# Attention and a gated two-layer network in one kernel: where the weight pieces stand in ScalarE's queue, and two flips ahead of two scores

## The chip, the core and the metric

The kernel runs on one core of one Trainium2 chip. The metric is the device time of one execution in microseconds, lower is better. The engines are TensorE (PE, its weight loads PEld), VectorE (DVE), ScalarE (ACT), GpSimd (POOL) and the queue that issues most transfers (SP).

## The reference

```python
# q, k, v: (8, 8, 576, 64) f32; block = 64, causal by blocks
scores = scale * np.matmul(q, k.transpose(0, 1, 3, 2))
scores = np.where(block_i >= block_j, scores, -1e9)
attn = np.exp(scores - np.max(scores, axis=-1, keepdims=True))
attn = attn / (np.sum(attn, axis=-1, keepdims=True) + 1e-09)
x = np.matmul(attn, v)            # then (B, H, S, D) -> (4608, 512)
h = x @ w_in                      # (512, 2048)
g = h * (1.0 / (1.0 + np.exp(-1.702 * h)))
out = g @ w_out                   # (2048, 512), f32
```

The weights come in as 64-bit floats.

## The kernel before

**Attention.** The 64 (batch, head) pairs are taken two at a time, in 32 turns n = 0 to 31 (and a last one that only finishes). `HP` is 4, so turns 0 to 3 are the first batch and the fifth turn is n = 4. A turn cuts the 576 rows of queries into five chunks (0 of 64 rows, 1 to 4 of 128). `load` fetches q and k, `prep` transposes them on DVE (L297). `score` multiplies them on PE into PSUM banks, then for each chunk DVE adds the mask and takes the row maxima (`weigh`, L351), ACT takes the exponential and its row sums (L358), DVE turns the sums into factors (L368, L371) and POOL multiplies (L376). In the first eight turns the weights are transposed by `flip` on PE (L102) and copied back by ACT (L411, L424). `av` multiplies them with the values on PE; ACT copies the sums of values to `xr` (L451, L450).

**The list of a turn.** `ORDER`, `START` (for n = 4) and `HANDOVER` (n = 8) are lists of items: `1+0`, `2/3`, `4` are scores of those chunks of head pair n, `a` is the flip of chunks 0 and 1 of n, `B` the flip of chunks 2 and 3 of n - 1, `C` the flip of chunk 4 of n - 1, `V` is `av(n - 1)`, `L` is `prep(n + 1)`, and `-` is nothing. After each item `convert` and `advance` are called.

**The weights.** 32 pieces of 128 x 512 are made from 64-bit words to a high and a low part. `load_weights` fetches a piece, `begin` lets ACT write its low words, scaled, to the one PSUM bank of tag `w3` (L219), `merge` is three DVE instructions (L223, L229, L234), and `split_weights` is ACT's cast to the high part (L243) and POOL's subtraction for the low part (L82). `begin` of the next piece needs that bank back, so it waits for L234 of this one. `convert` is called with a target from `WEIGHTS_BY`, in half steps: an even one is `merge`, an odd one is `split_weights` of this piece, the load of another and `begin` of the next.

**The network.** `moe` takes 12 tiles of 384 rows of `xr`: `split` makes high and low parts (ACT L498, DVE L82), 16 column groups each multiply with `w_in`, pass the gate (ACT L562, DVE L563, ACT L571, POOL L82) and multiply with `w_out`. The first tile waits for the sums of the first four head pairs, which are complete after `V` of the fifth turn. `advance` hands out its PE work by the position of the turn.

**What orders the queues.** A scheduler in the framework places each engine's instructions when the program is built: the earliest in program order of those that it reckons ready. The chip then runs each engine's list in that order. `keep_in_program_order` puts an instruction behind the one that was traced just ahead of it on its engine; it doesn't hold back what comes later. All PE work is pinned so, and the first three loads of pieces. PSUM banks are handed out in rotation by `bank()`: seven before the network starts.

Of the kernel before, what the change touches and what calls it, by code (L numbers as in the profile page):

```python
# [13 lines left out]
AF = mybir.ActivationFunctionType  # L14
# [15 lines left out]
)  # L30

START = "1+0 - B 2/3 L C - V - 4 - a - - -"
HANDOVER = "B C - 3+0/2+1 - - V - - - 4 - - L - -"


WEIGHTS_BY = ((0, 0), (8, 13), (14.5, 32))
TILES_BY = ((8.4, 0), (17.7, 1), (33.7, 4), (65.7, -2))

# [2 lines left out]
def attention_moe_kernel(  # L41
# [9 lines left out]
    nc = tc.nc  # L51
    B, H, S, D = q.shape
# [11 lines left out]
    HP = H // 2  # L64
# [6 lines left out]
    def f(ap):  # L71
        return ap.bitcast(F32)
# [5 lines left out]
    def phase(n):  # L78
        return 0 if n < HP else 1 if n < 2 * HP else 2

    def subtract(eng, out, in0, in1):
        eng.tensor_tensor(out=out, in0=in0, in1=in1, op=ALU.subtract)  # L82
# [3 lines left out]
    turns = {"n": 0, "bank": 0, "experts": False}  # L86
# [37 lines left out]
    def weights(name, g):  # L124
        if (name, g) not in home:
            home[name, g] = room(f"{name}{g}", [P, 4, WC], F32R, name)
        return home[name, g]
# [33 lines left out]
    for i in range(NCH):  # L161
        w, o = BLK * (2 * i + 1), 2 * BLK * i * i
# [12 lines left out]
    pieces = []  # L175
# [11 lines left out]
    def load_weights(upto):  # L187
        while conv["loaded"] < min(upto, len(pieces)):
            j = conv["loaded"]
            if j < 2 * len(places):  # L190
                if j % 2 == 0:
                    pair_of[j // 2] = room(places[j // 2], [P, 2, 2 * WC], U32, "words")
                at = [pair_of[j // 2][:, j % 2]]
            else:
                at = [
                    room("e1", [P, WC], U32, "wst") if j % 2 and x
                    else d2.tile([P, WC], U32, tag="osb", name="wst", bufs=3)
                    for x in range(2)
                ]
            n = 2 * WC // len(at)  # L200
            for x, w in enumerate(at):
                d = nc.sync.dma_start(out=w, in_=pieces[j][0][:, x * n : (x + 1) * n])
                if j < 3:
                    tc.keep_in_program_order(d)
            parts[j] = [
                (w.rearrange("p (c t) -> p c t", t=2), slice(x * n // 2, (x + 1) * n // 2))
                for x, w in enumerate(at)
            ]
            conv["loaded"] += 1
# [3 lines left out]
    bits, whole = {}, {}  # L213

    def begin(j):

        bits[j] = ps.tile([P, 512], F32, tag="w3", name="wm")
        for w, c in parts[j]:
            nc.scalar.activation(out=bits[j][:, c], in_=f(w[..., 1]), func=AF.Copy, scale=2.0**-112)  # L219

    def merge(j):
        u = bits.pop(j).bitcast(U32)
        nc.vector.tensor_scalar(  # L223
            out=u, in0=u, scalar1=3, scalar2=None, op0=ALU.logical_shift_left
        )

        z = whole[j] = room("e1" if j % 2 and j < 2 * len(places) else "wm", [P, WC], U32, "wm")
        for w, c in parts[j]:
            nc.vector.scalar_tensor_tensor(  # L229
                out=u[:, c], in0=w[..., 1], scalar=0x80000000, in1=u[:, c],  # L230
                op0=ALU.bitwise_and, op1=ALU.bitwise_or,
            )
        for w, c in parts.pop(j):
            nc.vector.scalar_tensor_tensor(  # L234
                out=z[:, c], in0=w[..., 0], scalar=29, in1=u[:, c],
                op0=ALU.logical_shift_right, op1=ALU.bitwise_or,
            )

    def split_weights(j):
        _, name, g, x = pieces[j]  # L240
        z = whole.pop(j)
        hi, lo = (weights(name + p, g)[:, x] for p in "hl")
        nc.scalar.copy(out=hi, in_=f(z))  # L243
        subtract(nc.gpsimd, lo, f(z), f(hi))

    def convert(upto):

        while conv["step"] < int(2 * upto):
            j, odd = divmod(conv["step"], 2)
            if odd:  # L250
                split_weights(j)
                if j + 1 < len(pieces):
                    load_weights(j + 3)
                    begin(j + 1)
            else:
                if j == 0:
                    begin(0)
                merge(j)
            conv["step"] += 1
# [201 lines left out]
    def order(n):  # L461
        return {HP: START, 2 * HP: HANDOVER}.get(n, ORDER[phase(n)]).split()

    def step(n):

        turns["n"] = n
        now = n < NPAIR

        def item(x):
            if x == "V":  # L470
                return (lambda: av(n - 1)) if n else None
            if x == "L":
                return (lambda: prep(n + 1)) if n + 1 < NPAIR else None
            if x in ("a", "B", "C"):
                m, chunks = {"a": (n, [0, 1]), "B": (n - 1, [2, 3]), "C": (n - 1, [4])}[x]
                return (lambda: flip(m, chunks)) if m >= 0 else None
            return (lambda: score(n, [[int(z) for z in y.split("+")] for y in x.split("/")])) if now and x != "-" else None

        return [item(x) for x in order(n)]
# [29 lines left out]
    def moe():  # L509
# [24 lines left out]
        for t in range(NT):  # L534
# [6 lines left out]
            for fc in range(NFC):  # L541
                if t == 0:
                    convert(fc // FG * GROUP + NDC + fc % FG + 1)
# [38 lines left out]
    def quota(pos):  # L582
        xs, ys = zip(*TILES_BY)
        return -1.0 if pos < xs[0] else np.interp(pos, xs, [ends[y if y >= 0 else y - 1] for y in ys])
# [7 lines left out]
    def advance(heads_done, until):  # L592

        while not state["done"] and not (until() and (state["gate"] or turns["n"] <= 2 * HP)):
            if state["wait"] is not None:
                if heads_for(state["wait"]) > heads_done:
                    return
                state["wait"] = None
            got = next(mo, None)
            if got is None:  # L600
                state["done"] = True
            elif isinstance(got, tuple):
                if got[0] == "tile":
                    state["wait"] = got[1]
                else:
                    state["gate"] = True
            else:
                state["gate"] = False
                state["t"] += got
# [14 lines left out]
    for n in range(NPAIR + 1):  # L624
        items = step(n)
        for sl, fn in enumerate(items):
            if fn is not None:
                fn()
            if order(n)[sl] == "V":
                heads_done = 2 * n  # L630
            pos = 2 * (n + (sl + 1) / len(items))
            convert(min(len(pieces), np.interp(pos - 0.5, *zip(*WEIGHTS_BY))))
            lim = quota(pos)
            advance(heads_done, lambda: state["t"] >= lim)
    advance(2 * NPAIR, lambda: False)
# [29 lines left out]
```

## Time and profile before

| what | value |
|---|---|
| runs | 1115.9, 1118.8 and 1119.08 us, median 1118.8 |
| span of the profiled execution | 1116.9 us |
| PE busy | 1082.2 us, 97% |
| PEld, DVE, ACT, POOL busy | 82%, 52%, 45%, 36% |
| mean granted TensorE clock | 0.988 |

The profile gives the span from the first to the last instruction of one execution. What lay around it in that execution isn't listed; the span is within the spread of the runs, 1.9 us under their median. A matmul's end is modelled, so PE's busy time is an upper bound. The granted clock is a share of 2.4 GHz, and 0.50 is 1.2 GHz.

### The profile page before, as it was taken

Reading aid. Unit: us, or ns where it says so; the run is one execution under the profiler, and the core shown is the slowest. Engines: PE = TensorE matmul, PEld = TensorE weight load, DVE = VectorE, ACT = ScalarE, POOL = GpSimd, SP = SyncE. Lnnn points to the kernel's source line nnn. Section 1 sums busy time; section 2 is a strip of 40 time slices with the busy share of each in tenths; the row PEclk is TensorE's granted clock in tenths of the full one; section 3 lists DMA queues with packets and bytes.
Section 4 is the critical chain, followed back from the end, with each engine's and each line's share of the span. In section 5 each row is a group of like instructions: output and inputs, shape, how many; then the busy total and the mean of one; then the engine's idle time right before and its main releaser. Section 6 shows DMA issues by size and latency. Waiting matters only on the chain. (4 is left out here: it accounts for less than half of the span.)

```text
span 1116.9 us, 19972 instructions
## 1 busy us (share of the span) xinstructions
PE 1082.2 (97%) x6960; PEld 912.9 (82%) x6960; DVE 584.2 (52%) x1856; ACT 498.9 (45%) x1321; POOL 406.4 (36%) x509
## 2 busy tenths in 40 slices
PE   6979999999999999999999999999999999999998
PEld 4757777788888888888888888888888888899997
DVE  6786786655645645655555555645645654211210
ACT  5865775443533534534443443443444434322322
POOL 4665565332333333333333332333333333122222
PEclk8979999999999999999999999999999999999999
DMA  8634523342434433243443333344442332200000
GB/s 183 193 89 153 146 61 80 72 103 59 96 81 86 109 80 70 58 99 71 113 86 75 80 92 68 63 108 86 86 103 66 71 84 54 54 30 1 29 1 29
DMA packets 219365, 91.25 MB, mean 82 GB/s; under 512 B 197760, under 2 KB 197760, under 8 KB 219264
## 3 DMA queue, kind: packets, MB, share of 16 engines
q1 hardware_dynamic: 214528, 89.38, 34.1%
q8 instruction: 55, 0.90, 0.3%
q10 hardware_dynamic: 4736, 0.59, 0.3%
q14 instruction: 46, 0.38, 0.1%
HBM read 45.09 MB, written 9.44 MB: 49 GB/s over the span
## 5 line engine op out<-in xcount | busy, mean ns | idle before, releaser
L82 POOL TENSOR_TENSOR gl<-g,gh 128x384 fp32r<-128x384 f32 x192 | 194.5, 1013 | 555.1 <-ACT gh L571 450.4
L563 DVE SCALAR_TENSOR_TENSOR g<-g,hp 128x384 f32<-128x384 f32 x192 | 106.0, 552 | 318.6 <-ACT g L562 317.2
L99 PE MATMUL hp<-xh,wih 128*128 128x384 f32 x768 | 265.8, 346 | 2.8 <-DVE g L563 1.8
L562 ACT ACTIVATE g<-hp 128x384 f32<-128x384 f32 x192 | 94.2, 491 | 368.5 <-PE hp L99 361.0
L99 PE MATMUL hp<-xh,wil 128*128 128x384 f32 x768 | 258.7, 337 | 0.0
L99 PE MATMUL hp<-xl,wih 128*128 128x384 f32 x768 | 254.4, 338 | 0.2
L99 PE MATMUL acc<-woh,gh 128*128 128x512 f32 x576 | 233.9, 406 | 0.0
L99 PE MATMUL acc<-wol,gh 128*128 128x512 f32 x576 | 227.0, 394 | 0.0
L99 PEld LDWEIGHTS hp<-xh,wih 128*128 128x128 f32 x768 | 144.4, 188 | 30.9 <-DVE g L563 20.3
L99 PE MATMUL acc<-woh,gl 128*128 128x512 f32 x576 | 168.2, 393 | 0.3 <-POOL gl L82 0.3
L571 ACT CAST gh<-g 128x384 fp32r<-128x384 f32 x192 | 98.4, 513 | 156.8 <-DVE g L563 156.5
L99 PEld LDWEIGHTS hp<-xh,wil 128*128 128x128 f32 x768 | 144.6, 188 | 5.6
L358 ACT ACTIVATE e<-e,mx 64x64 f32<-64x64 f32 (+4 forms) x240 | 132.2, 552 | 32.2 <-DVE mx L351 32.2
L376 POOL TENSOR_TENSOR e<-e,sm 64x64 f32<-64x64 f32 (+1 forms) x192 | 113.6, 612 | 86.3 <-DVE sm L371 42.5
L99 PEld LDWEIGHTS hp<-xl,wih 128*128 128x128 f32 x768 | 144.0, 188 | 1.0 <-DVE xl L82 1.0
L99 PE MATMUL bank<-qk 64*128 64x320 f32 (+4 forms) x768 | 124.3, 432 | 16.2 <-DVE qk L297 10.4
L99 PEld LDWEIGHTS acc<-woh,gh 128*128 128x128 f32 x576 | 108.2, 188 | 34.2 <-issue 10.8
L99 PEld LDWEIGHTS acc<-woh,gl 128*128 128x128 f32 x576 | 107.6, 188 | 25.4 <-POOL gl L82 1.2
L351 DVE CUSTOM_DVE_ANT_0 e<-bank,mask 64x64 f32<-64x64 f32 (+4 forms) x240 | 89.7, 417 | 70.1 <-PE bank L99 67.0
L99 PEld LDWEIGHTS acc<-wol,gh 128*128 128x128 f32 x576 | 108.4, 188 | 16.8 <-issue 0.4
L385 DVE STREAM_TRANSPOSE turned<-e 128x384 f32<-128x384 f32 (+1 forms) x192 | 92.5, 500 | 49.5 <-POOL e L376 48.9
L99 PEld LDWEIGHTS bank<-qk 64*128 64x128 f32 x768 | 71.4, 196 | 56.4 <-issue 25.4
(50 smaller groups left out, 960.6 us busy)
## 6 DMA issues: line engine op xcount, KB each, us to landing
turned<-turned SPq DMA_DIRECT2D x192, 80.0 KB, 2.1
turned<-turned SPq DMA_DIRECT2D x96, 112.0 KB, 2.2
raw<-in_q_dram SPq DMA_DIRECT2D x128, 72.0 KB, 2.3
out_dram<-osb SPq DMA_DIRECT2D x36, 256.0 KB, 2.4
raw<-in_k_dram SPq DMA_DIRECT2D x120, 72.0 KB, 2.4
turned<-turned SPq DMA_DIRECT2D x96, 88.0 KB, 2.1
words<-in_moe_w_in_dram SPq DMA_DIRECT2D x16, 512.0 KB, 5.6
vp<-in_v_dram SPq DMA_DIRECT2D x60, 128.0 KB, 2.4
```

The source lines that it names most:

```text
L82: eng.tensor_tensor(out=out, in0=in0, in1=in1, op=ALU.subtract)
L99: return tc.keep_in_program_order(nc.tensor.matmul(**kw))
L351: nc.vector.tensor_tensor_reduce(out=e[0:m, hd, lo:hi], in0=s, in1=mk, op0=ALU.add, op1=ALU.min, scale=-0.125, scalar=3e38 if lo == 0 else ...
L358: nc.scalar.activation(out=e[0:m, hd], in_=e[0:m, hd], func=AF.Exp, scale=-1.0, bias=mx[0:m, i, hd : hd + 1], accum_out=sm[0:m, i, hd : hd ...
L376: nc.gpsimd.tensor_tensor(out=x, in0=x, in1=sc.to_broadcast([m, width(i)]), op=ALU.mult)
L385: nc.vector.transpose(out=tw[:, :, SLOT[i] : SLOT[i] + i, hd].rearrange("p b j c -> p j b c"), in_=e[:, hd, 0 : i * P],)
L562: nc.scalar.activation(out=g, in_=hp[:, 0:tt], func=AF.Tanh, scale=1.702)
L563: nc.vector.scalar_tensor_tensor(out=g, in0=g, scalar=1.0, in1=hp[:, 0:tt], op0=ALU.add, op1=ALU.mult)
L571: nc.scalar.copy(out=gh, in_=g)
```

## The change

- `begin`'s ACT instructions are pinned behind what was traced ahead of them on ACT, in the turns n = 0 to 4.
- In an odd half step, the load and `begin` of the next piece are traced ahead of this piece's cast and subtraction.
- In turns 0 to 3 `convert` isn't called after the items 5 to 9 of the list (`L C - 4 -`), so what it would have done there comes after `V`.
- In the fifth turn `B` comes ahead of `1+0`, and the list has 16 items in place of 15.

```diff
-START = "1+0 - B 2/3 L C - V - 4 - a - - -"
+START = "B 1+0 - - 2/3 L C - V - 4 - a - - -"
+HELD = (5, 10)
@@ def begin(j):
         for w, c in parts[j]:
-            nc.scalar.activation(out=bits[j][:, c], in_=f(w[..., 1]), func=AF.Copy, scale=2.0**-112)
+            b = nc.scalar.activation(out=bits[j][:, c], in_=f(w[..., 1]), func=AF.Copy, scale=2.0**-112)
+            if turns["n"] <= HP:
+                tc.keep_in_program_order(b)
@@ def convert(upto):
             if odd:
-                split_weights(j)
                 if j + 1 < len(pieces):
                     load_weights(j + 3)
                     begin(j + 1)
+                split_weights(j)
@@ for n in range(NPAIR + 1):
             pos = 2 * (n + (sl + 1) / len(items))
-            convert(min(len(pieces), np.interp(pos - 0.5, *zip(*WEIGHTS_BY))))
+            if n >= HP or not HELD[0] <= sl < HELD[1]:
+                convert(min(len(pieces), np.interp(pos - 0.5, *zip(*WEIGHTS_BY))))
```

## Rows read from the trace of the kernel before

**Rows 1.** Windows: stretch and length, busy of PE, PEld, DVE, ACT, POOL, clock, DMA.

```profile
9.60:60.00 50.40, 42.50 (x362) 31.34 (x358) 40.23 (x151) 39.44 (x124) 30.68 (x44) 0.90 0.69 178
60.00:90.00 30.00, 23.69 (x138) 17.96 (x139) 22.08 (x51) 18.77 (x50) 17.52 (x19) 0.72 0.34 83
90.00:215.00 125.00, 116.48 (x805) 92.78 (x802) 90.95 (x265) 82.50 (x217) 69.49 (x77) 1.00 0.40 106
215.00:1116.90 901.90, 897.11 (x5650) 768.79 (x5648) 428.53 (x1381) 356.13 (x930) 286.14 (x359) 1.00 0.32 72
```

**Rows 2.** Waits of PE, 0 to 220: releaser, total us, times, longest.

```profile
PE bank L99 <- DVE qk L297: 10.4, 3, 7.1
...
PE bank L102 <- ACT xr L450: 2.1, 1, 2.1
```

**Rows 3.** Timeline of PE, 55 to 79: start, length, instruction, count, [idle before].

```profile
57.11 0.87 PE L102 MATMUL bank<-ident,turned 128*128 128x128 f32 x6
60.51 1.33 PE L99 MATMUL bank<-qk 64*128 64x192 f32 x8 [2.52 <-DVE qk L297]
...
64.98 2.37 PE L102 MATMUL bank<-ident,turned 128*128 128x128 f32 x10 [2.10 <-ACT xr L450]
68.16 3.87 PE L99 MATMUL bank<-qk 64*128 64x320 f32 x8 [0.82 <-ACT turned L424]
```

**Rows 4.** Timeline of ACT, 59 to 68.

```profile
59.73 0.62 ACT L243 CAST woh<-wm 128x512 fp32r<-128x512 f32 x1 [1.82 <-DVE wm L234]
60.26 0.63 ACT L219 ACTIVATE wm<-words 128x512 f32<-128x512 f32 x1
63.18 0.62 ACT L243 CAST woh<-wm 128x512 fp32r<-128x512 f32 x1 [2.29 <-DVE wm L234]
...
64.26 0.58 ACT L451 COPY xr<-bank 128x512 f32<-128x512 f32 x1
...
66.61 0.62 ACT L243 CAST woh<-wm 128x512 fp32r<-128x512 f32 x1 [0.98 <-DVE wm L234]
67.13 0.62 ACT L219 ACTIVATE wm<-words 128x512 f32<-128x512 f32 x1
67.69 0.42 ACT L424 COPY turned<-bank 64x128 f32<-64x128 f32 x2
```

**Rows 5.** Timeline of DVE, 59 to 65.

```profile
59.70 0.75 DVE L297 STREAM_TRANSPOSE qk<-raw 128x576 f32<-128x576 f32 x1
60.92 0.70 DVE L223 TENSOR_SCALAR wm<-wm 128x512 uint32<-128x512 uint32 x1 [0.47 <-ACT wm L219]
...
64.35 0.70 DVE L223 TENSOR_SCALAR wm<-wm 128x512 uint32<-128x512 uint32 x1 [1.21 <-ACT wm L219]
```

**Rows 6.** Timeline of SP, then of ACT: the third piece's load and first instruction.

```profile
22.68 0.97 SPq L202 DMA_DIRECT2D words<-in_moe_w_in_dram  x2
...
46.04 0.64 ACT L219 ACTIVATE wm<-words 128x512 f32<-128x512 f32 x1
```

**Rows 7.** DVE's idle before L223, whole run: releaser, us, times.

```profile
  ACT wm L219: 15.8, 18
```

**Rows 8.** Timeline of PE: the third turn's scores of chunks 2 and 3.

```profile
36.33 1.98 PE L99 MATMUL bank<-qk 64*128 64x320 f32 x8
```

**Rows 9.** Windows again: around the stretch at the lower clock.

```profile
57.00:60.30 3.30, 0.99 (x14) 0.65 (x8) 3.30 (x7) 1.48 (x6) 2.44 (x4) 1.00 0.00 0
60.40:73.90 13.50, 10.48 (x39) 7.32 (x40) 10.55 (x32) 10.23 (x32) 8.29 (x10) 0.50 0.75 183
74.00:80.00 6.00, 5.07 (x71) 4.34 (x69) 4.85 (x10) 4.03 (x10) 4.72 (x5) 1.00 0.01 3
200.00:206.00 6.00, 3.40 (x15) 1.87 (x14) 4.83 (x15) 1.58 (x5) 2.06 (x3) 1.00 0.11 25
```

**Rows 10.** Timeline of DVE: the subtractions of the first and the second tile.

```profile
77.66 3.50 DVE L82 TENSOR_TENSOR xl<-xr,xh 128x384 fp32r<-128x384 f32 x4
...
202.29 1.96 DVE L82 TENSOR_TENSOR xl<-xr,xh 128x384 fp32r<-128x384 f32 x4
```

## The prediction, made before the changed kernel was run

> **What bounds the kernel now.** I cut the span into stretches first [rows 1]. From 215 us on PE is busy 897.11 of 901.90 us: the change has nothing to win there, and as PE's work is the same before and after, a late start is carried through to the end one for one. So the change is worth what it does to PE's idle time ahead of 215 us, and to the stretches in which its clock is low. Between 9.6 and 60 us PE is idle for 7.90 us (50.40 - 42.50), between 60 and 90 for 6.31, between 90 and 215 for 8.52: 22.73 us in all, the most that any new order could return apart from the clock.
>
> Then the waits of PE say for whom [rows 2]: q and k transposed by DVE 10.4 us (7.1 of it the start of the kernel, which stays), and once 2.1 us the copy of sums of values on ACT. The timeline of PE places them [rows 3]. The flips of chunks 0 and 1 of the fourth turn begin at 57.11 and last 0.87. Then the fifth turn's first scores wait 2.52 us for DVE, `B`'s last ten transposes wait 2.10 us for L450, and the scores of chunks 2 and 3 wait 0.82 us for L424. This is the jam that the change is aimed at: 5.44 us of waits in 10 us.
>
> ACT's timeline shows why L450 was late [rows 4]. ACT stood at the cast of one piece until 59.73, at that of the next until 63.18 (2.29 us idle), and only at 64.26 came L451, the copy of sums that PE had finished before it began the flips at 57.11. L424 then waited behind another cast, which held ACT for 0.98 us. Each cast waits for DVE's L234, and DVE in turn waited 0.47 and 1.21 us for ACT's L219 [rows 5]. The two engines hand one piece back and forth, and the rest of their lists stands behind it.
>
> **The pins.** I work out which `begin` they bind. `WEIGHTS_BY` gives 13 pieces in 8 units of position, a turn is 2 units, so 6.5 half steps a turn: after the fourth turn the program has 24 half steps, 12 merges. The trace lags far behind. ACT's third L219 runs at 46.04, though its load went out at 22.68 [rows 6], and the one at 60.26 is the sixth [rows 4]. The program has the sixth `begin` in half step 10, late in the second turn (position 3.58); what it is pinned behind ran long ago. The L451 that was late belongs to the fourth turn. So as far as the lag stays, the pins and the held items leave the jam's order as it is, and I cost them at nothing. What hides them is the lag; if it goes (the first two pieces are moved behind the first turn's last scores, which may shift everything after), they would put the two casts and L219s behind L451. That is the first rival.
>
> **The next piece ahead of the cast.** When L234 ends, ACT now runs L219 first and the cast second. From the row, cast to L219 is 0.53 us (59.73 to 60.26) [rows 4]: L219 comes that much sooner, the cast 0.6 us later. It helps where DVE stands at L223 for ACT, which it does 18 times, 15.8 us in all [rows 7]. In the jam: the first such wait is 0.47 us, all of it saved, the second 1.21 us, of which 0.53 is saved [rows 5]. L451 comes 0.47 us sooner and L424, behind one more piece, 1.0 us sooner. The scores of chunks 2 and 3 wait for L424 last, so **1.0 us** on the path (bounds 0, if DVE fills the time with other work, and 2.1, if four pieces each pass on 0.53). The later waits of L223 lie where PE has the network's work; of these, some 14 waits at 0.53 us or 7.4 us of DVE time, I take **0.5 us**, since only the 8.52 us of idle after 90 us [rows 1] can return any of it; bounds 0 and 4. The later cast puts POOL's low parts off by 0.6 us; no wait of PE for them is among the rows, so nothing, with 0.6 as the other bound.
>
> **B ahead of 1+0.** Before, PE had nothing from 57.98 (57.11 + 0.87) to 60.51. `B` needs only the fourth turn's weights, so ten of its transposes can run in that hole, and the last four wait for L451, because the rotation of seven banks brings them to the bank of the sums (two for the sums, two for the flips, three for `B`, then again the first). The first scores come after them. They lose nothing that counts: they were computed by 61.84, but the next scores are released by L424 at 67.69 + 0.42 in any case [rows 3, 4]. So the 2.52 and 2.10 us aren't given back as such; they lie beside the wait for ACT. What is gained is that ACT can copy `B`'s flips, three banks that the scores of chunks 2 and 3 need next, ahead of the fifth turn's exponentials. At half clock eight such scores need some 3.96 us (twice the 1.98 of the third turn [rows 8]) against 3.87 seen, so hardly any of that time was a wait: I take **0.3 us**, bounds 0 and 0.82.
>
> **The clock.** Between 57.0 and 60.3 PE was busy for 0.99 of 3.30 us, and from 60.4 to 73.9 the granted clock was 0.50, with PE busy 10.48 us; then it is 1.00 again [rows 9]. With ten transposes in the hole, PE is busy more just ahead of the fall. But it then stands until L451, so the fall can come later and not be avoided. The eight scores at 68.16 took 3.87 us, the same in the third turn at full clock 1.98 [rows 3, 8]: 1.9 us for these alone. I take **1.5 us**, as the low stretch is likelier shortened than not; bounds 0 and 5.2 (half of 10.48).
>
> The Trainium skill, GPSIMD Engine Reference, "1. Specifications", says that GpSimd's SBUF interface is shared with VectorE, and that instructions with two SBUF inputs contend. The rows agree: four L82 subtractions on DVE took 3.50 us where POOL was busy 4.72 of 6 us, and 1.96 where it was busy 2.06 [rows 9, 10]. By it, a cast that comes later moves POOL's subtraction under other work of DVE, and the sum would be smaller by up to 1.5 us.
>
> **The sum.** 1.0 + 0.5 + 0.3 + 1.5 = 3.3 us less. The span is 1116.9; the sum gives 1113.6 for it. What lies around it isn't listed, so I take the sum from the median of the runs, 1.9 above the span: 1118.8 - 3.3 = **1115.5 us**.
>
> **Rivals.**
> - *The sums really go first.* If the moved first pieces end the lag, L451 follows PE at once. Then all of 5.44 us goes, and with it most of the low clock, 2.9 us if eight scores (1.9) and ten transposes (1.0, of 2.37) run at full clock: 8.3 us less, 1110.5. For it: ACT did stand 2.29 us at one cast [rows 4]. Against: the count of half steps above.
> - *Nothing that can be measured.* The 0.53 us per piece is eaten by the rest of DVE's list, which in 9.6 to 60 is busy 40.23 of 50.40 [rows 1], and the clock falls all the same: 1118.8, within 0.3%. (0.3%, 3.4 us, is about what a measurement of this kernel can tell from no change; the runs before lie 3.2 apart.)
> - *The quicker pieces take DVE from the attention.* Old pieces stand ahead of everything in the list. If one more is merged ahead of the fifth turn's q and k at 59.70 [rows 5], that costs three instructions of 0.70, 2.1 us, on the wait that was 2.52, and the first scores, which now come behind `B`, lose their slack. With subtractions that fall under POOL as in [rows 10], 1.5 us, it is 3.6 us: 1122.4. It decides once the scores of chunks 2 and 3 start later than 68.16. For it: DVE was busy 3.30 of 3.30 us ahead of them [rows 9]. Against: DVE then stood idle for 0.47 and 1.21 us in the jam [rows 5].
>
> The skill's rule on the shared interface belongs to the last of these; the trace so far shows it at the tiles' subtractions alone.
>
> **How the numbers follow.** My forecast has 0.42; its own range is 1112.5 to 1118, so half of it lies beyond 0.3% (0.22 faster, 0.20 same). The sums first: 0.20, faster. Nothing: 0.20, same. DVE taken: 0.18, slower. Faster 0.42, same 0.40, slower 0.18. The range goes from somewhat under the first rival's 1110.5, since the clock's bound is 5.2, to just short of the last rival's 1122.4: 1109 to 1122.
>
> **What would show it.** In the changed trace, each L219 ahead of its cast by some 0.6 us, and DVE's 15.8 us at L223 down by a third or more. In the jam: `B`'s first ten transposes ahead of 60.5, L451 at about 63.8 (at 58 by the first rival), L424 ahead of 67, scores of chunks 2 and 3 at about 67, and a low clock of less than 13.5 us. The first tile's first matmul comes some 2.8 us sooner. I am wrong if the scheduler, seeing pieces sooner, orders the third and fourth turns anew, so that PE's 7.90 us of idle ahead of 60 grow, or if the idle time after 90 us changes by more than what happens ahead of it.

## The result: 0.45% slower, and the profile after

Seven runs of the changed kernel have a median of 1122.45 us (1119.64 to 1126.71), seven of the kernel before 1118.8 (1115.9 to 1119.65): ratio 1.0045, interval 1.0031 to 1.0059. (The ratio is not that of the medians, which lie 3.65 us or 0.33% apart; it is the measure used throughout.) The forecast was 1115.5 us with a range of 1109 to 1122. The median is 3.65 us higher where a gain of 3.3 was forecast.

The profiled execution took 1122.59 us, with a span of 1120.8 (before 1116.9). In the changed kernel each line number is 1 to 3 higher: L82 is now L83, L219 is L220, L223 is L226, L234 is L237, L243 is L246, L376 is L379, L411 is L414, L424 is L427 and L451 is L454. The experiments shift them again by a few.

Windows of the changed kernel, columns as in [rows 1]:

```profile
9.60:60.00 50.40, 40.34 (x374) 30.37 (x371) 39.15 (x154) 40.67 (x128) 31.77 (x45) 0.93 0.68 179
60.00:90.00 30.00, 24.07 (x146) 18.66 (x145) 26.08 (x62) 19.54 (x52) 18.78 (x20) 0.77 0.32 83
90.00:215.00 125.00, 114.78 (x759) 90.98 (x758) 87.27 (x248) 78.07 (x208) 66.82 (x74) 0.95 0.39 102
215.00:1120.80 905.80, 900.82 (x5677) 771.79 (x5675) 429.60 (x1387) 357.83 (x933) 287.13 (x360) 1.00 0.32 72
```

Against [rows 1], the first two stretches have higher clocks (0.93 for 0.90, 0.77 for 0.72) and more instructions of PE done. The third has 759 matmuls in place of 805, 10.22 us of idle time in place of 8.52, and a clock of 0.95 where it was 1.00. So in these two profiles time is gained early and lost between 90 and 215 us.

**The jam is relieved.** Timeline of PE, the stretch of [rows 3]:

```profile
56.81 1.97 PE L103 MATMUL bank<-ident,turned 128*128 128x128 f32 x16
59.83 0.63 PE L103 MATMUL bank<-ident,turned 128*64 128x128 f32 x4 [1.06 <-ACT xr L454]
60.39 0.76 PE L100 MATMUL bank<-qk 64*128 64x192 f32 x8
63.19 3.40 PE L100 MATMUL bank<-qk 64*128 64x320 f32 x8 [2.03 <-ACT turned L427]
```

Timeline of ACT, the stretch of [rows 4]:

```profile
58.11 0.62 ACT L246 CAST woh<-wm 128x512 fp32r<-128x512 f32 x1 [0.93 <-DVE wm L237]
58.64 0.62 ACT L220 ACTIVATE wm<-words 128x512 f32<-128x512 f32 x1
59.20 0.58 ACT L454 COPY xr<-bank 128x512 f32<-128x512 f32 x1
61.65 0.63 ACT L220 ACTIVATE wm<-words 128x512 f32<-128x512 f32 x1 [1.08 <-DVE wm L237]
62.22 0.60 ACT L246 CAST woh<-wm 128x512 fp32r<-128x512 f32 x1
62.73 0.41 ACT L427 COPY turned<-bank 64x128 f32<-64x128 f32 x2
```

The flips of `a` and the first ten of `B` run in one row of 16 from 56.81. ACT takes up one cast and one L220 and then the sums, at 59.20; before, two such pairs stood ahead of L451 at 64.26. At 61.65 the new order shows: L220 0.57 us ahead of its cast (at 58.11 the scheduler still put a cast first). The waits of 2.52, 2.10 and 0.82 us are gone, one of 1.06 and one of 2.03 stand in their place. The scores of chunks 2 and 3 start at 63.19 (before 68.16), and the first matmul of the network at 74.66 (before 78.32). DVE's idle time ahead of L226, whole run, as in [rows 7]:

```profile
  ACT wm L220: 10.2, 13
```

It was 15.8 us in 18 times.

**The loss at the eighth turn's flips.** `B` and `C` flip the weights of the turn before, so the eighth turn's flips (head pair n = 7) stand at the head of the ninth turn's list. "Eighth" below means these flips. Timeline of PE of the changed kernel, from `B`'s ten to the scores that follow (the last nine belong to `C`):

```profile
178.14 1.25 PE L103 MATMUL bank<-ident,turned 128*128 128x128 f32 x10
181.39 0.63 PE L103 MATMUL bank<-ident,turned 128*64 128x128 f32 x4 [2.00 <-ACT turned L414]
184.33 2.18 PE L103 MATMUL bank<-ident,turned 128*128 128x128 f32 x9 [0.89 <-POOL turned L379]
189.29 1.78 PE L100 MATMUL bank<-qk 64*128 64x448 f32 x10
```

The same of the kernel before:

```profile
180.61 1.25 PE L102 MATMUL bank<-ident,turned 128*128 128x128 f32 x10
182.35 0.63 PE L102 MATMUL bank<-ident,turned 128*64 128x128 f32 x4 [0.49 <-ACT turned L411]
185.16 1.20 PE L102 MATMUL bank<-ident,turned 128*128 128x128 f32 x9 [0.78 <-POOL turned L376]
188.05 1.78 PE L99 MATMUL bank<-qk 64*128 64x448 f32 x10
```

From these flips to these scores it is 7.44 us before (188.05 - 180.61) and 11.15 after (189.29 - 178.14). The 2.47 us by which the flips start sooner than before become a lag of 1.24. The same nine flips take 1.20 us before and 2.18 after: the clock. Windows of the changed kernel, the two late stretches at the lower clock:

```profile
182.00:188.80 6.80, 5.92 (x21) 4.75 (x20) 1.19 (x4) 2.15 (x6) 3.56 (x4) 0.50 0.00 0
205.90:212.70 6.80, 6.43 (x17) 5.28 (x18) 4.83 (x15) 2.25 (x5) 0.99 (x1) 0.50 0.13 22
```

The granted clock is 0.50 (1.2 GHz) in both; in the trace of before it is 1.00 in both windows. What held the four flips at 181.39 up, ACT's timeline of the changed kernel shows:

```profile
179.18 0.38 ACT L220 ACTIVATE wm<-wst 128x256 f32<-128x256 f32 x1
179.50 0.61 ACT L246 CAST woh<-wm 128x512 fp32r<-128x512 f32 x1
180.01 0.51 ACT L574 CAST gh<-g 128x384 fp32r<-128x384 f32 x1
180.42 0.40 ACT L220 ACTIVATE wm<-wst 128x256 f32<-128x256 f32 x1
180.75 1.33 ACT L414 COPY turned<-bank 128x512 f32<-128x512 f32 x3
```

The same of the kernel before:

```profile
181.31 0.50 ACT L571 CAST gh<-g 128x384 fp32r<-128x384 f32 x1
181.71 1.07 ACT L411 COPY turned<-bank 128x512 f32<-128x512 f32 x2
182.67 0.64 ACT L243 CAST woh<-wm 128x512 fp32r<-128x512 f32 x1
```

Before, only the gate's cast stood ahead of the first copy of flips, which began 1.10 us after the flips (181.71 - 180.61). After, L220, the cast of the last piece but one, the gate's cast and another L220 do, and it begins 2.61 us after them.

But the wait that ends last is the one for POOL, ahead of the nine flips. They need two multiplications (L376, now L379). Timeline of POOL of the changed kernel:

```profile
179.83 1.15 POOL L379 TENSOR_TENSOR turned<-turned,sm 128x576 f32<-128x576 f32 x1 [3.88 <-DVE sm L374]
180.93 1.28 POOL L83 TENSOR_TENSOR wol<-wm,woh 128x512 fp32r<-128x512 f32 x1
182.16 1.01 POOL L83 TENSOR_TENSOR gl<-g,gh 128x384 fp32r<-128x384 f32 x1
183.12 1.15 POOL L379 TENSOR_TENSOR turned<-turned,sm 128x576 f32<-128x576 f32 x1
```

The same of the kernel before:

```profile
181.89 1.01 POOL L82 TENSOR_TENSOR gl<-g,gh 128x384 fp32r<-128x384 f32 x1 [2.66 <-ACT gh L571]
182.85 2.25 POOL L376 TENSOR_TENSOR turned<-turned,sm 128x576 f32<-128x576 f32 x2
```

After the change the piece's subtraction (its low part, 1.28 us) and the gate's stand between the two multiplications. The second ends at 184.27, and the nine flips start 6.19 us after the ten (184.33 - 178.14), before 4.55 (185.16 - 180.61). So by these rows a quicker copy on ACT alone would not have let them start sooner; PE would have waited longer for POOL.

**The ninth turn.** From its scores of 64x256 to those of 64x448 PE takes 11.73 us before (201.29 to 213.02) and 14.54 after (202.54 to 217.08), with a wait of much the same length, 2.60 and 2.50 us; after it the clock fell in the changed kernel's profile and not in the other. The account of the two profiles: 2.47 ahead at the flips, 3.71 lost there, 2.81 in the ninth turn, together 4.05 behind; the spans differ by 3.9. Of these, only the 3.71 are shown to be the change's. e5 below runs the instructions of every engine in the order of the kernel before. Its profile has the fall of the ninth turn, and its flips start at 177.38, 3.23 us sooner than in the profile of before and 0.76 sooner than in that of the changed kernel. Window of e5:

```profile
203.90:207.20 3.30, 3.30 (x12) 3.30 (x11) 2.54 (x7) 0.49 (x2) 0.00 (x0) 0.50 0.28 45
```

So two executions of one order differ by more than the 2.47 us at the flips, and by 1.56 us in the ninth turn (13.29 in e5, 11.73 before). How much of the 2.47 and the 2.81 us is the change's isn't shown.

### The profile page after: what moved, and what is told of

It reads as the page before. It is cut to its first block, busy times and chain, and to the rows that moved or that the text cites. A ratio compares the mean times of both kernels' runs of the same rounds, so it can differ in the third digit from the quotient of the medians.

```text
span 1120.8 us, 19999 instructions
## 1 busy us (share of the span) xinstructions
PE 1082.3 (97%) x6960; PEld 913.7 (82%) x6960; DVE 584.4 (52%) x1856; ACT 498.0 (44%) x1321; POOL 407.1 (36%) x509
## 5 line engine op out<-in xcount | busy, mean ns | idle before, releaser
L83 POOL TENSOR_TENSOR gl<-g,gh 128x384 fp32r<-128x384 f32 x192 | 194.4, 1012 | 548.5 <-ACT gh L574 444.9
L379 POOL TENSOR_TENSOR e<-e,sm 64x64 f32<-64x64 f32 (+1 forms) x192 | 113.6, 612 | 89.1 <-ACT e L361 42.4
L100 PE MATMUL bank<-qk 64*128 64x320 f32 (+4 forms) x768 | 122.0, 427 | 16.5 <-DVE qk L300 9.8
```

The costliest lines, as they stand in the source:

```text
L100: return tc.keep_in_program_order(nc.tensor.matmul(**kw))
L379: nc.gpsimd.tensor_tensor(out=x, in0=x, in1=sc.to_broadcast([m, width(i)]), op=ALU.mult)
```

## The experiments

"Swap" below is the next piece's load and `begin` ahead of the cast, "pins" and "held" the edits of `begin` and of `HELD`, "flips" that of `START`. Edits are given against the kernel before where nothing else is said. All results stand in one table, since one number decides most of them: "network" is the start of its first matmul, "flips" that of the eighth turn's ten flips, "eighth" the time from these to the scores of 64x448 behind them, and "ninth" that from the ninth turn's scores of 64x256 to the next of 64x448, both start to start in the profile.

| kernel | median us (runs) | ratio, interval | mean clock | network | flips | eighth | ninth |
|---|---|---|---|---|---|---|---|
| before | 1118.8 (7) |  |  | 78.32 | 180.61 | 7.44 | 11.73 |
| changed | 1122.45 (7) | 1.0045, 1.0031 to 1.0059 | 0.985 | 74.66 | 178.14 | 11.15 | 14.54 |
| e1 swap | 1125.06 (6) | 1.0069, 1.0052 to 1.0086 | 0.985 | 78.80 | 182.92 | 10.70 | 14.39 |
| e2 flips | 1117.69 (12) | 1.0004, 0.9994 to 1.0014 | 0.989 | 76.37 | 176.71 | 7.44 | 13.26 |
| e3 pins, held | 1115.56 (11) | 0.9985, 0.9976 to 0.9995 | 0.992 | 73.75 | 177.14 | 7.45 | 14.45 |
| e4 swap early | 1117.37 (12) | 0.9996, 0.9986 to 1.0007 | 0.990 | 74.50 | 178.44 | 7.44 | 14.42 |
| e5 pins | 1117.31 (11) | 0.9996, 0.9986 to 1.0005 | 0.989 | 77.03 | 177.38 | 7.44 | 13.29 |
| e6 held | 1116.72 (11) | 0.9985, 0.9975 to 0.9996 | 0.991 | 73.41 | 178.06 | 7.44 | 14.63 |
| e7 swap late | 1116.20 (11) | 0.9983, 0.9972 to 0.9994 | 0.990 | 76.85 | 178.77 | 7.44 | 11.63 |
| e8 fill | 1119.17 (11) | 1.0014, 1.0000 to 1.0027 | 0.991 | 73.7 | 176.78 | 10.55 | 11.62 |
| e9 cast pinned | 1116.19 (11) | 0.9978, 0.9969 to 0.9987 | 0.990 | 74.78 | 177.07 | 6.89 | 13.19 |
| e10 held, fill | 1114.65 (8) | 0.9967, 0.9956 to 0.9978 | 0.994 | 73.3 | 178.05 | 7.44 | 11.73 |
| e11 fill alone | 1116.77 (12) | 0.9991, 0.9982 to 1.0001 | 0.990 | 76.6 | 177.18 | 7.44 | 11.73 |
| e12 cast, fill | 1115.35 (9) | 0.9978, 0.9969 to 0.9987 | 0.992 | 74.9 | 177.18 | 6.89 | 11.65 |

Each ratio is to runs of the kernel before on the same chip (medians there 1117.84 for e1 to e4, 1118.24 for e5 to e8, 1117.69 for e9 to e12). "Network", "flips" and "ninth" have a chance part: e5, e7 and e11, which have the order of before up to there, start the network 1.3 to 1.7 us sooner than it in their profiles, and e5 and e11 the flips 3.2 to 3.4 us sooner. "Eighth" has none of it: it is 7.44 or 7.45 in all nine kernels in which the first copy of flips and both of POOL's multiplications run ahead of the piece's cast and subtraction there.

**e1: the swap alone.**

```diff
             if odd:
-                split_weights(j)
                 if j + 1 < len(pieces):
                     load_weights(j + 3)
                     begin(j + 1)
+                split_weights(j)
```

> Alone of the change: load and begin of the next piece ahead of the cast, in all turns. Theory A (the change wins some 4 us around the fourth and fifth turn and loses more at 172 to 215 us, because with the quicker chain a cast and an L219 stand ahead of flip copies in the eighth turn, PE waits longer and its clock falls): first matmul of the network 2 to 4 us sooner than before, then a loss of some 4 to 7 us at 172 to 215 with one or two stretches at half clock, in all 0 to 4 us slower than before. Rival B (the loss comes from the fifth turn's list, B first and 16 items): 1 to 3 us faster than before, no half clock after 100 us. Rival C (chance: the clock falls by its own phase in any kernel): within 0.3% of before, half-clock stretches differ from run to run.

Ratio 1.0069: the swap alone is slower than the whole change. It wins nothing in the jam: from the first copy of sums to the fourth turn's it is 31.2 us (33.6 to 64.8), before 31.1 (33.1 to 64.3). Its network starts 1.8 to 2.2 us later than in e5, e7 and e11. The eighth turn's flips show the same loss as in the changed kernel. Timeline of PE of e1:

```profile
182.92 1.25 PE L102 MATMUL bank<-ident,turned 128*128 128x128 f32 x10
186.17 0.63 PE L102 MATMUL bank<-ident,turned 128*64 128x128 f32 x4 [2.00 <-ACT turned L411]
189.12 2.07 PE L102 MATMUL bank<-ident,turned 128*128 128x128 f32 x9 [1.52 <-POOL turned L376]
193.62 1.78 PE L99 MATMUL bank<-qk 64*128 64x448 f32 x10
```

It is the same 2.00 us wait, without the flips, pins or held items, and the nine flips start 6.20 us after the ten, when POOL is done, as in the changed kernel (6.19). This stretch gives 3.26 us of e1's loss (10.70 - 7.44). Its flips start 2.31 us later than before and 5.5 later than in e5; what it loses there was not taken apart.

**e2: the flips alone.**

```diff
-START = "1+0 - B 2/3 L C - V - 4 - a - - -"
+START = "B 1+0 - - 2/3 L C - V - 4 - a - - -"
```

> Alone of the change: the fifth turn's list with B first and 16 items. Theory A: 0 to 2 us faster than before, no loss at 172 to 215. Rival B: 3 to 5 us slower than before, the loss at 172 to 215 here. Rival C: within 0.3%.

Ratio 1.0004: nothing that can be measured. The flips run in the hole, and then PE waits. Timeline of PE of e2:

```profile
57.27 0.77 PE L102 MATMUL bank<-ident,turned 128*128 128x128 f32 x5 [0.56 <-POOL turned L376]
63.01 1.06 PE L102 MATMUL bank<-ident,turned 128*64 128x128 f32 x4 [4.98 <-ACT xr L451]
```

The two waits of [rows 3] have become one of 4.98 us for the sums: they lay beside the wait for ACT, as the prediction had it.

**e3: pins and held items; e5: pins alone; e6: held items alone.**

```diff
 e3, e5
-            nc.scalar.activation(out=bits[j][:, c], in_=f(w[..., 1]), func=AF.Copy, scale=2.0**-112)
+            b = nc.scalar.activation(out=bits[j][:, c], in_=f(w[..., 1]), func=AF.Copy, scale=2.0**-112)
+            if turns["n"] <= HP:
+                tc.keep_in_program_order(b)
 e3, e6
+HELD = (5, 10)
-            convert(min(len(pieces), np.interp(pos - 0.5, *zip(*WEIGHTS_BY))))
+            if n >= HP or not HELD[0] <= sl < HELD[1]:
+                convert(min(len(pieces), np.interp(pos - 0.5, *zip(*WEIGHTS_BY))))
```

> Alone of the change: L219 pinned in turns 0 to 4, and no weights after the items 5 to 9 in turns 0 to 3. By my count of half steps (the lag makes the pins idle) ACT's order in the fourth turn stays and the time is within 2 us of before. If the pins bind: L451 of the fourth turn right behind PE, at 58 instead of 64, and 4 us or more gained by the first tile.

> Of the last but one pair of edits alone the pins of L219. Theory A: what relieves the fourth turn is that the first two pieces move, and the pin alone does that too (it puts the first L219 behind the exponentials of the first turn's last chunk): copy of sums of the fourth turn at 59 to 60 in place of 64.3, first matmul of the network 3 to 5 us sooner, 1114 to 1118 in all. Rival: the held items do it, and this one is as before, copy at 64, 1117 to 1119.

> The held items alone. By theory A as before (copy of sums of the fourth turn near 64, 1117 to 1119), since L219 of the first piece can still float up; by the rival this one has the copy at 59 to 60 and 1114 to 1117.

e3 and e6 both come to 0.9985, e5 to 0.9996 with 1 in its interval. Timeline of ACT of e5:

```profile
61.51 0.62 ACT L245 CAST woh<-wm 128x512 fp32r<-128x512 f32 x1 [2.29 <-DVE wm L236]
62.03 0.62 ACT L219 ACTIVATE wm<-words 128x512 f32<-128x512 f32 x1
62.59 0.58 ACT L453 COPY xr<-bank 128x512 f32<-128x512 f32 x1
```

With pins alone no engine's order differs from before: ACT still stands 2.29 us at the second cast, and the sums come behind it. So e5 also serves as a second profile of the order before. Timeline of ACT of e6:

```profile
58.23 0.62 ACT L244 CAST woh<-wm 128x512 fp32r<-128x512 f32 x1 [1.22 <-DVE wm L235]
58.76 0.63 ACT L220 ACTIVATE wm<-words 128x512 f32<-128x512 f32 x1
59.33 0.58 ACT L452 COPY xr<-bank 128x512 f32<-128x512 f32 x1
```

With the held items alone the second pair is behind the sums. So it is they that relieve the jam. But of the 3.2 to 3.6 us by which e6's network starts sooner than in e5, e7 and e11, nothing is left at the flips (178.06, and 177.38 in e5).

**e4: the changed kernel, with the swap only up to the fifth turn.** Against the changed kernel:

```diff
             if odd:
+                ahead = turns["n"] <= HP
+                if not ahead:
+                    split_weights(j)
                 if j + 1 < len(pieces):
                     load_weights(j + 3)
                     begin(j + 1)
-                split_weights(j)
+                if ahead:
+                    split_weights(j)
```

> The whole change, but the next piece goes ahead of the cast in turns 0 to 4 alone; later the cast is first, as before. Theory A: the lead of some 3.5 us at the first tile stays, no loss at 172 to 215: 1113 to 1116. Rival B: like the changed kernel, 1121 to 1124. Rival C: 1115 to 1123, whatever the order.

Ratio 0.9996. The first wait at the eighth turn's flips is 0.50 us again and the stretch 7.44, while the network still starts at 74.50. Taking the swap from the late turns undoes the loss. It doesn't leave a gain: with the whole of the change's early part e4 can't be told from before.

**e7: the kernel before, with the swap only from the seventh turn on (n from 6).**

```diff
             if odd:
-                split_weights(j)
+                late = turns["n"] >= 6
+                if not late:
+                    split_weights(j)
                 if j + 1 < len(pieces):
                     load_weights(j + 3)
                     begin(j + 1)
+                if late:
+                    split_weights(j)
```

> The kernel before, with the next piece ahead of the cast from the seventh turn (n = 6) on alone. Theory A (the loss of the changed kernel at 172 to 198 comes from the order of the last pieces): PE's wait for flip copies in the eighth turn grows from 0.49 to about 2 us, and 2 to 5 us slower than before. If the early pieces have to run ahead for that (the chain must arrive sooner): within 1 us of before.

Ratio 0.9983, "eighth" 7.44. That the late order alone does the harm is wrong. That e7 is 0.17% faster than before, with the jam as it was, was not expected and stays unexplained; it is as much as e3 and e6 gain. Timeline of ACT of e7:

```profile
179.89 0.58 ACT L415 COPY turned<-bank 128x512 f32<-128x512 f32 x1
180.37 0.41 ACT L219 ACTIVATE wm<-wst 128x256 f32<-128x256 f32 x1
180.70 0.61 ACT L243 CAST woh<-wm 128x512 fp32r<-128x512 f32 x1
```

The flips start at 178.77 here, and the copy is placed ahead of the L219 and the cast. The reading is that the harm needs both: late pieces with L219 first, and a chain of pieces that the swap of the earlier turns has brought forward, so that these instructions are placed ahead of the copy. It is argued from e1, e4 and e7; the sixth turn (n = 5), which has the swap in neither e4 nor e7, was not tried by itself.

**e9: the changed kernel, with one more pin, on the cast of the last piece but one.** Against the changed kernel:

```diff
-        nc.scalar.copy(out=hi, in_=f(z))
+        h = nc.scalar.copy(out=hi, in_=f(z))
+        if j == 30:
+            tc.keep_in_program_order(h)
```

> The changed kernel with one line: the cast of the last piece but one is pinned behind what was traced ahead of it on ACT. This moves that cast and the last one behind flip copies of the eighth turn, and their subtractions on POOL behind multiplications; DVE's, PE's and SP's orders stay. Theory A2 (the loss at 172 to 198 is these two casts and L219s ahead of the flip copies): PE's waits in the eighth turn are 2 us shorter, no half clock at 182 to 189, lead at 198 as at 168: 1118 to 1120, 3 to 4 us less than the changed kernel. Rival D (the loss there comes from the clock's phase or from the pieces arriving sooner): 1121.5 to 1123.5.

Only the last two casts and their subtractions change places. The ratio falls from 1.0045 to 0.9978, more than was expected. Timeline of ACT of e9:

```profile
178.12 0.38 ACT L220 ACTIVATE wm<-wst 128x256 f32<-128x256 f32 x1
178.44 0.58 ACT L416 COPY turned<-bank 128x512 f32<-128x512 f32 x1
179.66 0.61 ACT L246 CAST woh<-wm 128x512 fp32r<-128x512 f32 x1
```

The copy is now ahead of the cast, and on POOL the two multiplications run in one row from 178.76 to 181.01, ahead of both subtractions. PE waits 0.75 and 0.50 us in place of 2.00 and 0.89, the clock doesn't fall here, and the stretch takes 6.89 us in place of 11.15. So the places of the last two casts and their subtractions cost 4.26 us here; what is ACT's share and what POOL's, e9 doesn't separate, as it moves both. The rest of the difference of 6.3 us between the medians is not placed: in the profiles e9's flips start 1.07 us sooner and its fall of the ninth turn is shorter (13.19 us in place of 14.54), though no instruction ahead of the flips differs.

**e8: the changed kernel with matmuls by zero, meant for the holes.** Fourteen in the eighth turn (n = 7) and twelve in the ninth, into an accumulator of the network; they add zeros. Against the changed kernel (`live["acc"]` is the accumulator that is open):

```diff
+    def filler(count):
+        for _ in range(count):
+            mm(out=live["acc"][:, 0:384], lhsT=mask[:, 0:P], rhs=mask[:, 0:384], start=False, stop=False)
@@ score, ninth turn, ahead of the fifth chunk's
+                        if n == 2 * HP and i == 4 and lo and not hd:
+                            filler(12)
@@ flip of head pair n = 6, in the eighth turn
+                    if n == 6 and chunks == [4] and not x + y:
+                        filler(5)
+        if n == 6 and chunks == [2, 3]:
+            filler(9)
```

> The changed kernel with 26 more matmuls of zeros on PE, added to sums in acc, placed where PE waits in the eighth turn (9 and 5) and in the ninth (12). Theory A, clock: PE is busy in its waits, the clock stays at 1.00 from 182 to 213, and 3 to 6 us come back although PE has some 4.5 us more work: 1117 to 1120, mean clock 0.988 or more. If the clock isn't what costs, the time is that of the changed kernel or more, 1122 to 1127.

Ratio 1.0014. In the ninth turn the fall is gone and the stretch is 11.62 us. The fourteen missed their hole: they stand among the flips of head pair 6 and ran at 152.44 and 158.87, more than 15 us ahead of the wait, which is at the flips of pair 7. There the wait is still 1.71 us, the clock falls, and the stretch is 10.55. A few instructions of ACT, DVE and POOL changed places in these turns too. So whether matmuls in that wait would keep the clock up was not tested.

**e10, e11, e12: the twelve matmuls of the ninth turn alone**, put into e6, into the kernel before and into e9. The edit is the ninth turn's part of e8.

> The held items alone, with 12 matmuls of zeros on PE, added to sums in acc, in PE's wait of the ninth turn. Orders of the other engines stay. Theory A, clock: the fall after 202 us doesn't come, and 1.5 to 3 us of the 2.9 that were lost there come back: 1113.5 to 1115.5. If the fall there has another cause than PE's wait: 1116 to 1118.

> The kernel before with the same 12 matmuls of zeros in the ninth turn. Theory A, clock: it falls there in part of its runs, so the median comes down by 1 to 2.5 us, to 1116 to 1117.5, and the slowest runs (0.986) go. Otherwise 1118 to 1119.5.

> The changed kernel with the pinned cast and the 12 matmuls of zeros. If the two late losses are all that stands between the change and its early lead of 2.5 to 4 us: 1114.5 to 1116.5, 1 to 2 us ahead of the kernel before with the same filler less than that. If the early lead is lost in any case: as the changed kernel, 1120 or more.

e10 is the best version, 1114.65 us, 0.9967 (0.9956 to 0.9978): 0.33% faster than the kernel before. Apart from the twelve matmuls all engines have the order of e6. Window of e6 from the ninth turn's wait on:

```profile
202.10:209.00 6.90, 6.42 (x17) 5.27 (x18) 4.94 (x16) 2.25 (x5) 1.00 (x1) 0.51 0.13 21
```

Window of e10, the same place:

```profile
202.00:209.00 7.00, 6.68 (x32) 5.48 (x32) 6.39 (x19) 4.43 (x10) 1.14 (x2) 1.00 0.13 21
```

The clock is 1.00 for 0.51 and PE does 32 matmuls for 17: the ninth stretch is 11.73 us for 14.63. e11 (0.9991) and e12 (0.9978, as e9) show less: neither can be told from the kernel that it was put into, though the ninth stretch is short in both.

## Why the prediction was wrong

**The step that failed** is the one on the later waits of L223: "I take 0.5 us, since only the 8.52 us of idle after 90 us can return any of it; bounds 0 and 4". It counted only what a quicker chain of pieces returns. It had no bound for what it costs where the pieces end. At the eighth turn's flips the new order has a cast and two L220s of the last pieces ahead of ACT's first copy of flips, and a subtraction of theirs between POOL's two multiplications. PE waits 2.00 us for 0.49, and then for POOL, and the clock falls behind the first of these waits. Of the 3.71 us lost there, 1.64 lie ahead of the nine flips, which start when POOL is done (6.19 us after the ten, for 4.55); the other 2.07 lie behind them, where PE has no wait and does the same work at the lower clock. Counted by PE's waits it is 1.24 us more idle time (2.89 for 1.65, the waits of 2.00 and 0.89 against those of 0.49, 0.38 and 0.78) and 2.47 of slower work. Three runs carry this: e1 shows the loss with the swap alone, e4 its end when the late turns have the old order, e9 its end when one cast, and with it the subtraction, comes later. e7 corrects the simple form of it: the late order alone, without the swap in the earlier turns, costs nothing. The stretch doesn't give all of the change's loss: e4 and the changed kernel differ by 0.49% in ratio, some 5.5 us, and 3.71 of these are placed.

**The gain that was forecast ahead of it didn't come either.** The terms of the jam make 2.8 us (1.0 + 0.3 + 1.5). e4, which has all of the early change without the late loss, is at 0.9996 (0.9986 to 1.0007), at most 1.6 us faster than before. The jam is relieved, but when `av` of the fifth pair starts, the changed kernel's profile (111.06) is no longer ahead of e5's (110.80), as it was by 2.37 us at the network. Where these went was not taken apart.

**The signs.** Of those that the prediction named, PE's idle ahead of 60 us did grow, from 7.90 to 10.06 us, but with more matmuls done at a higher clock (0.93 for 0.90), so it is no measure of the loss. Idle after 90 us rose by 1.70, no more than the 1.78 ahead of it (2.16 more up to 60, 0.38 less up to 90): the sign was set on idle time, and more than half of the late loss is clock. The prediction gave these signs no price and no chance.

**The other steps:**

- *Next piece ahead of the cast, 1.0 us in the jam*: mis-sized, as far as e1 shows. e1 gives 0 there, the lower bound. DVE's wait at L223 did fall by a third, from 15.8 to 10.2 us, as foretold.
- *Pins cost nothing, because of the lag*: right. e5 has every engine's order as it was.
- *Held items cost nothing, because of the lag*: wrong. The half steps of turns 0 to 3 that they put off include a pair that stood ahead of the sums; e6 has L452 at 59.33, and its network starts at 73.41, 4.9 us sooner than in the profile of before and 3.2 to 3.6 sooner than in those of e5, e7 and e11. In the whole time it is -0.15%, no more than e7 has without it. The count of half steps looked at what `begin` is pinned behind and not at which casts come later. Which of the four turns does it was not tried.
- *`B` ahead of `1+0`, 0.3 us*: within what e2 can tell (0.9994 to 1.0014). That the 2.52 and 2.10 us lie beside the wait for ACT was right.
- *The clock, 1.5 us, bounds 0 and 5.2*: not shown. The stretch of 13.5 us at 0.50 is 6.8 now, as forecast, but one of 3.4 us from 84.2 before is 6.8 from 76.2, and e5, with the order of before, has a first one of 13.6 us and no second. So the changed kernel has no less time at 0.50 there than e5 has. That the clock is also lost late, 6.8 us at 0.50 at the eighth turn's flips, was not in the sum.
- *The later cast puts POOL's low parts off, nothing*: the cost is elsewhere. PE doesn't wait for a low part, but one of 1.28 us stands ahead of a multiplication for which PE waits. PE's waits for POOL are shorter, 0.89 us for 0.38 and 0.78, only because it comes to them later. That the last of them ends 1.64 us later after the ten flips was not in the prediction.
- *POOL's subtraction under other work of DVE, up to 1.5 us*: little of it. The first tile's four subtractions on DVE take 3.73 us before (1.35 and 1.28 while POOL is busy, 0.55 and 0.55 while it isn't) and 4.15 after (0.56, 1.29, 1.28 and 1.02), and PE waits 0.55 us for the last. It is no part of the late loss, which is POOL's own order.

**The rivals.** *The sums really go first* describes the jam best: L454 at 59.20, near its 58, and one pair ahead of it in place of two; it is the held items that do it (e6). Its 8.3 us did not come: PE still waited 1.06 and 2.03 us, and the network started 3.66 us sooner than in the profile of before and 1.9 to 2.4 sooner than in those of e5, e7 and e11. *The quicker pieces take DVE from the attention* has the right sign and nearly the time, 1122.4, by luck: its mechanism isn't there. The scores of chunks 2 and 3 start at 63.19, not later than its 68.16, and the queues that the pieces take are ACT's and POOL's, 110 us later.

**Its parts add up** roughly: +0.69% (e1), +0.04% (e2) and -0.15% (e3) make +0.58%, and the whole change measured +0.45%.

**What stays open.** What the rest of the change's loss is, beyond the 3.71 us. Why e7 gains 0.17% and e9 0.22%. How ACT and POOL share the loss at the flips. The fall in the ninth turn comes and goes between executions of one order: of ten profiles without matmuls by zero there, eight have it (stretches of 13.19 us and more) and two, before and e7, have none, and e5, with the order of before, has it. In which share of a kernel's executions it comes isn't known; so why e10 gains 2.0 us on e6 with the filled wait (0.9967 against 0.9985), and e11 at most 2.0 on before (0.9 by the medians), is open too.

## What to carry to other kernels

When a chain of background work is made quicker, look where it will end, and at what stands in the in-order queues of all its engines there: it lost 3.7 us 110 us behind the jam, and its gain in the jam can't be measured in the whole time. Try the parts of a bundled change one by one; here one of four may be worth a gain (held items, -0.15%), two nothing that can be measured, and one is a loss (+0.69%). On a kernel in which PE is 97% busy, compare two traces by the start times of the same instruction along the whole run: the lead that is gained and lost again names the places to look, where the shares of busy time (97% in both) say nothing. Then take a second profile of one order, as e5 is here by chance: it tells which of these differences are the change's. And where several waits follow each other, ask which one ends last; here it was POOL's, and not the longest.

## What the runs showed of the chip

- Waits of PE of 1.7 to 2.6 us in a busy stream were followed by 3.4 to 6.8 us at a granted clock of 0.50 in most profiles: at the eighth turn's flips in all three that have such a wait there (in e1 and e8 with one of 1.52 or 0.66 behind it), in the ninth turn in eight of ten. The slower work then cost more than the added idle time: 2.47 us against 1.24 at the changed kernel's flips. Waits of 0.38 to 0.78 us at the flips were followed by no fall.
- With twelve matmuls by zero in 2.1 us of the ninth turn's wait the clock stayed at 1.00 in all four profiles that had them (e8, e10, e11, e12).
- The times of one kernel's runs go mostly with the clock: among 30 runs of the kernel before, eight at a mean clock of 0.986 took 1118.95 to 1120.54 us, three at 0.991 took 1116.32 to 1116.56, about 0.6 us for each 0.001. So a difference of one profile of 2 us is not yet one of two kernels; at the same instruction the profiles of before and e5, of one order, are up to 3.2 us apart.
